# The opening of a three-stage kernel: the first block's words split in PSUM, eight weight tails by identity products, attention in finer stages

## The chip, the cores and the metric

The kernel runs on one core of a Trainium2 chip. Times are device microseconds of one launch. TensorE (PE in the profile), VectorE (DVE), ScalarE (ACT), GpSimd (POOL) and SyncE (SP, which only issues transfers here) each work through a queue of their own in order; semaphores hold an instruction until what it needs is there. The metric is the launch time, the median over several runs.

## The reference

```python
for t in range(S):                                       # B=4, H=8, S=768, D=48
    state = alpha[:, :, t, :, None] * state + einsum('bhd,bhe->bhde', k[:, :, t], v[:, :, t])
    y[:, :, t] = einsum('bhd,bhde->bhe', q[:, :, t], state)
x = y.transpose(0, 2, 1, 3).reshape(3072, 384)
out = 0                                                  # four experts, 384 -> 1024 -> 384
for e in range(4):
    out += (probs[:, e:e+1] / sum(probs)) * (maximum(x @ w1[e], 0) @ w2[e])
h = out @ w_in                                           # 384 -> 2048 -> 384
return (h - tanh(h)) @ w_out
```

A gated linear attention makes 3,072 rows of 384 features; four experts and then one larger layer are applied to every row. All of it is float32.

## The kernel before

**Words in two parts.** The large products run in a rounded 32-bit format, so every operand is split into a high part (the rounded word) and a low part (word minus high part), and a product is three: high by high, low by high, high by low. A weight tile of an expert (`w`, 128 by 768, one for each of the eight hidden slices f) is split by `w_prep`: ACT rounds it (line 425) and POOL subtracts (line 426). Attention's small products keep plain float32, which the trace records as two matmuls each.

**Attention.** Work is cut into 24 units (128 time steps of one batch entry). A unit is: two scans over the gates on DVE (`st_c`, line 260, and `st_r`, line 270), the scaled queries and keys (`st_prod`, 280), transposes and scores on PE (303 and 308), the key copy on ACT (315), the mask on DVE (322), the state update and the outputs on PE (333, 341, 344; the first four units have no state yet and use 348), the copy of the outputs (376), their store to DRAM as `xr` on ACT's queue (381), and the state's update on DVE and POOL (356, 358, 365, 367). `st_flag` takes a range check of the scans on ACT (290). A table, `STAGES`, gives each piece an offset; `points` walks through it, four points to a unit, and so writes the order in which the engines get the pieces.

**The first expert and the attention run together.** `steps0` is expert 0 over the rows in blocks: 256, 256, then five of 512. A step is one block and one f: `mm1` (line 589, 9 matmuls into `ph`), then ReLU and split by `evac1` (ACT 596, DVE 597), then `mm2` (line 641, 9 matmuls into three `po` banks), which is issued one step later (`flush(1)`). Between the two halves of a step the loop issues some points of attention, enough that the units of the next block are ready in time. `x_load` fetches a block of rows from DRAM (`xraw`), `x_parts` splits it on ACT and DVE (520, 521).

**The opening.** Before the loop: 20 matmuls on zeros (`busy`) keep PE occupied, units 0 and 1 run alone, their outputs go to DRAM by line 381 and come back as the first block. In between stand `w_prep(0)` to `w_prep(3)` and more `busy` matmuls; `w_prep(4)` to `w_prep(7)` are issued in the first four steps of the loop.

**The rest** (experts 1 to 3 in paired blocks, then the last layer) is not touched, but for one list that is emptied between the two (`phs`, which picks PSUM banks).

Of the kernel before, what the change touches and what calls it, by code (L numbers as in the profile page):

```python
# [183 lines left out]
def tile_kernel(ctx: ExitStack, tc: tile.TileContext, qka, a0, v, vT, pT, w12, w64, out):  # L184
# [34 lines left out]
    ident = const.tile([112, 112], F32, name="ident", tag="ident")  # L219
# [53 lines left out]
    def st_scan(u):  # L273
        st_c(u)
        st_r(u)

# [21 lines left out]
    def st_scores(u):  # L298
        s = unit[u]
        if u < NU - B:  # L300
            s["pt"] = bank(u, [P, 448], 0)
            for j in range(4):
                nc.tensor.transpose(s["pt"][:, j * 112:(j + 1) * 112],  # L303
                                    s["prod"][:, 512 + j * C:512 + (j + 1) * C], ident)
# [21 lines left out]

    def st_out(u):
        s = unit[u]
        heads = [(j, hf, r, slice((2 * j + hf) * D, (2 * j + hf + 1) * D)) for j in range(4) for hf, r in halves()]
        if u < NU - B:  # L330
            s["pu"] = bank(u, [112, 4, D], 0)
            for j, hf, r, h_ in heads:
                nc.tensor.matmul(s["pu"][r, j], s["kt"][:, j * 112 + 64 * hf:j * 112 + 64 * hf + D], s["vt"][:, h_],  # L333
                                 start=True, stop=True)
# [10 lines left out]
        else:  # L345
            for j, hf, r, h_ in heads:
# [3 lines left out]
    def st_upd(u):  # L350
        s = unit[u]
        if u < NU - B:
            for hf, r in halves():
# [3 lines left out]
                else:  # L357
                    nc.vector.tensor_copy(sd, s["pu"][r])
# [10 lines left out]
    def st_y(u):  # L369
        s = unit[u]  # L370
        s["y"] = at.tile([112, 512], F32, name="y", tag="y", bufs=2)
        for hf, r in halves():
            if u < 2 and hf:
                nc.vector.tensor_copy(s["y"][r], s["py"][r])
            else:
                nc.scalar.copy(s["y"][r], s["py"][r])

    def st_store(u):
        s = unit[u]
        for hf, r in halves():  # L380
# [5 lines left out]
    STAGES = [(st_out, 9), (st_scores, 3), (st_kt, 4), (st_mask, 4), (st_upd, 10), (st_y, 10), (st_store, 10),  # L386
              (st_state, 11), (st_scan, 0), (st_prod, 1), (st_flag, 2), (st_load, 2)]
# [12 lines left out]
    def ready(u):  # L400
        return 4 * (u - 2) + 11
# [21 lines left out]
    def w_parts(w, t):  # L423
        wh, wl = (w[:, k].rearrange("p a n -> p (a n)") for k in range(2))
        nc.scalar.copy(wh, t)
        nc.gpsimd.tensor_tensor(out=wl, in0=t, in1=f32(wh), op=ALU.subtract)
# [75 lines left out]
    blocks0 = [(0, 256), (256, 256)] + [(t, 512) for t in range(512, NT, 512)]  # L502
# [20 lines left out]
    def x_keep(t0, n):  # L523
        o, i = t0 % 512, t0 // 512
        nc.sync.dma_start(out=xs[i][:, :, i % 2:, o:o + n], in_=f32(xt[0, t0][:, :, i % 2:, :n]))
# [225 lines left out]
    with tc.manual_schedule():  # L751
        a_load(0)
        qk_load(0)
        nc.sync.dma_start(out=a0s, in_=a0)
        a_load(1)
        v_load(0)
        qk_load(1)
        w_load(0)
        v_load(1)
# [4 lines left out]
        v_load(2)  # L764
        w_load(3)
        a_load(3)
        qk_load(3)
        v_load(3)
        pr = at.tile([P, NE, 24], F32, name="pr", tag="pr")
        nc.sync.dma_start(out=pr, in_=pT.rearrange("e (p j) -> p e j", p=P))  # L770
        w_load(4)
# [13 lines left out]
        make_identity(nc, ident)  # L785
        make_upper_triangular(nc, mask)
        for t in state + sbd:
# [18 lines left out]

        st_c(0)
# [3 lines left out]
        w_prep(0)  # L811
        st_scores(0)
        st_kt(0)
        st_mask(0)
# [10 lines left out]
        busy(4)  # L825
        st_out(1)
        st_y(1)
        st_store(1)
        x_load(0, 0, 256)
        w_load(5)  # L830
        w_load(6)
        w_load(7)
        st_upd(0)
        st_upd(1)
        st_flag(0)
        busy(10)
        points(2)
        st_flag(1)
        w_prep(2)
        for kb in range(KB):  # L840
            x_parts(0, 256, kb)
        points(3)
        w_prep(3)
# [212 lines left out]
```

## Time and profile before

| | |
|---|---|
| runs | 1322.45, 1323.63, 1318.81 us (median 1322.45) |
| profiled execution, its own time | 1320.48 us |
| its span, first to last instruction | 1318.7 us |
| busy: PE, DVE, ACT, POOL | 97%, 69%, 46%, 41% |
| TensorE clock granted, mean | 0.986 of full speed |

A `PE` row is matrix work, `PEld` a weight load beside it. The granted clock is the share of full speed that TensorE was given: 1.00 is 2.4 GHz and 0.50 is 1.2 GHz, its two levels. Rows of the timeline merge instructions of one kind; what stands in square brackets is how long the engine had been idle before the row, and on what.

### The profile page before, as it was taken

The page shows a single profiled execution, that of the slowest core. Times are in us where ns is not written, and L with a number is a line of the kernel's source. Part 1 is how long each engine was busy: PE and PEld are TensorE (multiplying, and loading weights), DVE is VectorE, ACT ScalarE, POOL GpSimd, SP SyncE. Part 2 cuts the span into 40 slices and gives each one's busy share as a digit, 9 for nine tenths or more (in the row PEclk, how much of TensorE's full clock was granted, in tenths as well). Part 3 has the DMA queues.
Part 4 walks back from the last instruction along what each step waited for, and adds up shares of the span by engine and source line. Part 5 has one row for each costly group of instructions (what it writes and reads, how often), then busy time and mean ns, then how long its engine had stood idle before and what let it go on. Part 6 is the DMA issues. An engine that isn't in the chain of part 4 may idle for free.

```text
span 1318.7 us, 18568 instructions
## 1 busy us (share of the span) xinstructions
PE 1285.5 (97%) x6748; PEld 1051.6 (80%) x6748; DVE 906.7 (69%) x1383; ACT 610.0 (46%) x1096; POOL 536.8 (41%) x487
## 2 busy tenths in 40 slices
PE   6799999999999999999999999999999999999997
PEld 3788888888788887888888888888888888888885
DVE  7678667624456767776667766655878787878785
ACT  3343333323443324333333433334776767677764
POOL 3311110003433225522134521215787776767664
PEclk8789999999999999999999999999999999999999
DMA  7465543425662636471626261519100000000000
GB/s 245 121 164 167 163 127 120 149 64 174 226 209 102 221 109 208 125 239 44 215 71 233 88 204 64 191 53 346 50 25 1 25 0 25 0 25 0 25 1 28
DMA packets 86389, 153.24 MB, mean 116 GB/s; under 512 B 7568, under 2 KB 43664, under 8 KB 86032
## 3 DMA queue, kind: packets, MB, share of 16 engines
q1 hardware_dynamic: 76304, 147.24, 33.8%
q10 hardware_dynamic: 9984, 4.72, 1.4%
q8 instruction: 55, 0.90, 0.3%
q14 instruction: 46, 0.38, 0.1%
HBM read 115.71 MB, written 36.23 MB: 115 GB/s over the span
## 4 chain that ended last, share of the span: by engine, by line
PE 88%; DVE 4%; issue 2%; DMA 2%; ACT 1%; POOL 1%; SPq 0%; DVEq 0%; POOLq 0%; ACTq 0%
PE po L641 42%; PE ph L674 20%; PE ph L589 20%; PE pa L308 2%; PE pa L341 1%; PE pa L344 1%; DVE fg L260 1%; DMA xt<-xs 1%; PE pa L303 1%; DMA xraw<-xr 1%; PE pa L333 1%; DVE hl L597 0%; DVE prod L280 0%; DMA wraw<-w 0%; DVE fg L270 0%
## 5 line engine op out<-in xcount | busy, mean ns | idle before, releaser
L641 PE MATMUL po<-hh,w 128*128 128x512 f32 (+1 forms) x1776 | 450.5, 389 | 0.0
L641 PEld LDWEIGHTS po<-hh,w 128*128 128x128 f32 x1776 | 327.3, 189 | 73.9 <-issue 3.5
L589 PE MATMUL ph<-xt,w 128*128 128x512 f32 (+1 forms) x1368 | 327.0, 385 | 0.3 <-DVE ptmp L663 0.3
L589 PEld LDWEIGHTS ph<-xt,w 128*128 128x128 f32 x1368 | 251.9, 192 | 52.7 <-issue 1.2
L641 PE MATMUL po<-hl,w 128*128 128x512 f32 (+1 forms) x888 | 247.2, 386 | 1.2 <-DVE hl L621 1.2
L674 PE MATMUL ph<-xt,w 128*128 128x512 f32 x864 | 233.9, 392 | 1.3 <-DVE hl L597 0.9
L641 PEld LDWEIGHTS po<-hl,w 128*128 128x128 f32 x888 | 165.3, 189 | 35.8 <-DVE hl L621 1.6
L674 PEld LDWEIGHTS ph<-xt,w 128*128 128x128 f32 x864 | 162.4, 188 | 37.7 <-DVE hl L597 1.3
L597 DVE SCALAR_TENSOR_TENSOR hl<-ph,hh 128x512 fp32r<-128x512 f32 (+1 forms) x128 | 84.1, 657 | 143.8 <-ACT hh L596 143.7
L596 ACT ACTIVATE hh<-ph 128x512 fp32r<-128x512 f32 (+1 forms) x128 | 73.2, 572 | 237.0 <-PE ph L589 143.5
L75 POOL TENSOR_SCALAR gmk<-gu 128x512 int32<-128x512 f32 x96 | 143.3, 1493 | 48.8 <-ACT gu L71 48.1
L621 POOL TENSOR_TENSOR hl<-gg,hh 128x512 fp32r<-128x512 f32 x94 | 122.0, 1298 | 54.1 <-ACT hh L619 54.1
L479 POOL TENSOR_TENSOR wo<-wf,wo 128x384 fp32r<-128x384 f32 x32 | 35.1, 1098 | 211.1 <-ACT wo L478 211.1
L702 ACT COPY ut<-ph 128x512 f32<-128x512 f32 x108 | 63.4, 587 | 112.9 <-PE ph L674 112.5
L71 ACT ACTIVATE gu<-ph 128x512 f32<-128x512 f32 x96 | 57.7, 601 | 114.7 <-PE ph L589 69.7
L667 POOL TENSOR_TENSOR acc<-acc,ptmp 128x512 f32<-128x512 f32 x51 | 64.9, 1297 | 112.3 <-DVE ptmp L663 112.3
L674 PE MATMUL ph<-xt,ws 128*128 128x512 f32 x324 | 104.6, 395 | 1.2 <-DVE ph L736 1.2
L76 DVE SCALAR_TENSOR_TENSOR ghu<-ph,gu 128x512 f32<-128x512 f32 x96 | 66.3, 690 | 54.2 <-ACT gt L72 53.8
L80 DVE COPY_PREDICATED gg<-gmk,ph 128x512 f32<-128x512 int32 x96 | 71.9, 749 | 10.1 <-POOL gmk L75 0.3
L365 POOL TENSOR_TENSOR state<-state,fc 112x192 f32<-112x192 f32 x20 | 10.1, 506 | 168.6 <-DVE state L356 145.0
L79 DVE SCALAR_TENSOR_TENSOR gg<-gs,ghu 128x512 f32<-128x512 f32 x96 | 66.4, 692 | 12.7
L674 PEld LDWEIGHTS ph<-xt,ws 128*128 128x128 f32 x324 | 60.9, 189 | 15.8 <-DVE ph L736 2.3
(121 smaller groups left out, 1524.5 us busy)
## 6 DMA issues: line engine op xcount, KB each, us to landing
xt<-xs SPq DMA_DIRECT2D x54, 512.0 KB, 6.1
xt<-xb SPq DMA_DIRECT2D x27, 512.0 KB, 5.8
r<-w SPq DMA_DIRECT2D x32, 384.0 KB, 5.8
w64s<-wo SPq DMA_DIRECT2D x32, 384.0 KB, 3.1
w<-w64s SPq DMA_DIRECT2D x16, 768.0 KB, 6.3
qk<-qka SPq DMA_DIRECT2D x24, 448.0 KB, 6.3
wraw<-w SPq DMA_DIRECT2D x26, 384.0 KB, 3.9
pb<-pn SPq DMA_DIRECT2D x23, 256.0 KB, 4.4
```

The costliest lines, as they stand in the source:

```text
L75: nc.gpsimd.tensor_scalar(out=mk, in0=u, scalar1=T2, scalar2=None, op0=ALU.is_gt)
L76: nc.vector.scalar_tensor_tensor(out=hu, in0=ph, scalar=C4, in1=u, op0=ALU.mult, op1=ALU.mult)
L79: nc.vector.scalar_tensor_tensor(out=gg, in0=s2, scalar=B2, in1=hu, op0=ALU.add, op1=ALU.mult)
L80: nc.vector.copy_predicated(out=gg, mask=mk, data=ph)
L589: nc.tensor.matmul(ph[:, :n], w[:, a, 0, kb * P:(kb + 1) * P], x[:, b, kb, :n], start=m == 0, stop=m == len(seq) - 1)
L596: nc.scalar.activation(a[:, :n], ph[:, :n], AF.Relu)
L597: nc.vector.scalar_tensor_tensor(out=b[:, :n], in0=ph[:, :n], scalar=0.0, in1=f32(a[:, :n]), op0=ALU.max, op1=ALU.subtract)
L621: eng.tensor_tensor(out=b, in0=gg, in1=f32(a), op=ALU.subtract)
L641: nc.tensor.matmul(po[d, pool][:, :n], w[:, wi, 1, d * P:(d + 1) * P], r[:, :n], start=first and pi == 0, stop=last_ and pi == 2)
L667: nc.gpsimd.tensor_tensor(out=a_, in0=a_, in1=tmp, op=ALU.add)
L674: nc.tensor.matmul(ph, w[:, a], x[:, b], start=start and m == 0, stop=m == len(seq) - 1, skip_group_check=not start)
L702: nc.scalar.copy(t, ph)
```

## The change

Six edits, all in the opening and in the loop of expert 0:

1. The outputs of units 0 and 1 no longer go through DRAM before the first block. `place` copies parts of the values into a zeroed area (five small copies on ACT for a unit), so that `direct` can form the outputs with ten products whose rows are already in the order of the features; ACT rounds them out of PSUM into the high part, DVE subtracts into the low part, ACT copies them once more for the store that a later stage needs.
2. The low part of the eight weight tiles of expert 0 is made on PE: for each half of a tile, identity by the plain tile plus minus-identity by the high part, summed in PSUM; ACT copies the sum out. The POOL subtraction goes. `w_prep(0)` to `w_prep(2)` come before the loop, the other five in its first five steps.
3. The stages of attention are finer: the two scans stand at points 0 and 2 instead of both at 0, the products at 3, and everything behind one point later.
4. The blocks of expert 0 are four of 256 rows and four of 512; `mm2` is issued two steps behind `mm1`.
5. Small work moves: the gate of a unit's state (`fc`) from DVE to POOL, the first state copies from DVE to ACT, all output copies to ACT.
6. Loads are put in another order: the last four weight tiles are asked for before the loop, the row weights (`p_load`) in step 3, and rows are kept by one transfer for each of three parts.

```diff
-            nc.vector.tensor_tensor(out=s["fc"], in0=s["fg"].rearrange("p (j t) -> p j t", t=C)[:, 0:4, C - 1],
+            nc.gpsimd.tensor_tensor(out=s["fc"], in0=s["fg"].rearrange("p (j t) -> p j t", t=C)[:, 0:4, C - 1],
...
-                    nc.vector.tensor_copy(sd, s["pu"][r])
+                    nc.scalar.copy(sd, s["pu"][r])
...
+    def direct(u):
+        s = unit[u]
+        vz = spare(u * 480, 480)
+        py = bank(u, [P, 384], 1)
+        seen = {}
+        for (kb, h), (row, o) in PLACES.items():
+            a, b = max(48 * h, P * kb), min(48 * h + 48, P * kb + P)
+            w = s["vt"][:, a:b] if o is None else vz[:, o:o + (P if row == 0 else b - P * kb - row)]
+            n = seen[kb] = seen.get(kb, 0) + 1
+            nc.tensor.matmul(py[row:row + w.shape[1], kb * C:(kb + 1) * C], w,
+                             s["am"][h % 2][:, h // 2 * C:(h // 2 + 1) * C],
+                             start=n == 1, stop=True, skip_group_check=n > 1)
+        t = xt[0, 0][:, :, :, u * C:(u + 1) * C]
+        p3 = py.rearrange("p (k t) -> p k t", t=C)
+        nc.scalar.copy(t[:, 0], p3)
+        nc.vector.tensor_tensor(out=t[:, 1], in0=p3, in1=f32(t[:, 0]), op=ALU.subtract)
+        y = spare(960, 384).rearrange("p (k t) -> p k t", t=C)
+        nc.scalar.copy(y, p3)
+        nc.scalar.dma_start(out=xr[0].rearrange("(kb p) t -> p kb t", p=P)[:, :, u * C:(u + 1) * C], in_=y)
...
-    STAGES = [(st_out, 9), (st_scores, 3), (st_kt, 4), (st_mask, 4), (st_upd, 10), (st_y, 10), (st_store, 10),
-              (st_state, 11), (st_scan, 0), (st_prod, 1), (st_flag, 2), (st_load, 2)]
+    STAGES = [(st_out, 10), (st_scores, 4), (st_kt, 5), (st_mask, 5), (st_upd, 11), (st_y, 11), (st_store, 11),
+              (st_state, 12), (st_c, 0), (st_r, 2), (st_prod, 3), (st_flag, 3), (st_load, 3)]
...
-            w_parts(w, wraw.pop(i))
+            t = wraw.pop(i)
+            wh, wl = (w[:, k].rearrange("p a n -> p (a n)") for k in range(2))
+            nc.scalar.copy(wh, t)
+            for o in (0, 384):
+                pw = rolling(0)
+                nc.tensor.matmul(pw[:, 0:384], ident, t[:, o:o + 384], start=True, stop=False)
+                nc.tensor.matmul(pw[:, 0:384], negid, wh[:, o:o + 384], start=False, stop=True)
+                nc.scalar.copy(wl[:, o:o + 384], pw[:, 0:384])
...
-    blocks0 = [(0, 256), (256, 256)] + [(t, 512) for t in range(512, NT, 512)]
+    blocks0 = [(t, 256) for t in range(0, 1024, 256)] + [(t, 512) for t in range(1024, NT, 512)]
...
-        st_out(0)
-        st_y(0)
-        st_store(0)
+        update(0)
+        direct(0)
         st_scores(1)
         st_kt(1)
+        w_prep(0)
         st_mask(1)
-        w_prep(1)
-        busy(4)
-        st_out(1)
-        st_y(1)
-        st_store(1)
-        x_load(0, 0, 256)
...
+        st_flag(0)
+        points(3)
+        update(1)
+        direct(1)
+        w_prep(1)
+        st_flag(1)
+        points(4)
         st_upd(0)
         st_upd(1)
...
-        busy(10)
...
+        w_prep(2)
...
-            flush({5: 2, 6: 3, 7: 3}.get(f, 1) if last else 1)
+            flush({5: 2, 6: 3, 7: 3}.get(f, 1) if last else 2)
...
-                if bi == 0 and f < 4:
-                    w_prep(4 + f)
+                if bi == 0 and f < 5:
+                    w_prep(3 + f)
```

How PE's queue changes where the loop begins. First the kernel before: the last transposes and scores ahead of the loop (`pa` is an attention bank), then both first steps' `mm1` (18 matmuls into `ph`), then the first `mm2` into the `po` banks.

```order
L303 MATMUL pa<-ident,prod 128x112 x4
L308 MATMUL pa<-prod 128x128 x8
L589 MATMUL ph<-xt,w 128x256 x18
L641 MATMUL po_481<-hh,w 128x256
L641 MATMUL po_482<-hh,w 128x256
L641 MATMUL po_483<-hh,w 128x256
```

The same place in the changed kernel (`acc_88` and `acc_89` are where the plain weight tiles wait, line 631 is `mm1`, 300 and 305 are the transposes and scores):

```order
L463 MATMUL ph<-acc_88,ident 128x384
L464 MATMUL ph<-w,negid 128x384
L463 MATMUL ph<-acc_88,ident 128x384
L464 MATMUL ph<-w,negid 128x384
L631 MATMUL ph<-xt,w 128x256 x9
L300 MATMUL pa<-ident,prod 128x112 x4
L305 MATMUL pa<-prod 128x128 x8
L463 MATMUL ph<-acc_88,ident 128x384
L464 MATMUL ph<-w,negid 128x384
L463 MATMUL ph<-acc_88,ident 128x384
L464 MATMUL ph<-w,negid 128x384
L631 MATMUL ph<-xt,w 128x256 x9
```

The products that make the low parts of a weight tile now stand in PE's queue ahead of each early `mm1`, and the first `mm2` has gone back behind the third `mm1`.

How ACT's queue changes between the second unit's outputs and the first ReLU. Before (425 rounds a weight tile, 290 is the range check, 520 rounds the rows that came back from DRAM, 596 is the ReLU):

```order
L376 COPY y<-pa 48x512
L381 DMA xr_91<-y 48x4x128 x2
L290 ACTIVATE ab,flags<-fg 112x1024 x2
L425 CAST w<-acc_88 128x768
L520 CAST xt<-xraw 128x256 x3
L290 ACTIVATE ab,flags<-fg 112x1024
L425 CAST w<-acc_88 128x768
L596 ACTIVATE hh<-ph 128x256
```

After (410 and 413 read unit 1's outputs out of PSUM, 459 rounds a weight tile, 465 copies half a low part out of PSUM, 361 are state copies, 638 is the ReLU):

```order
L410 CAST xt<-pa 128x3x128
L413 COPY acc_87<-pa 128x384
L414 DMA xr_91<-acc_87 128x3x128
L459 CAST w<-wraw 128x768
L465 CAST w<-ph 128x384 x2
L287 ACTIVATE ab,flags<-fg 112x1024 x2
L361 COPY state_136<-po_286 48x192 x2
L361 COPY state_137<-pa 48x192 x2
L459 CAST w<-acc_88 128x768
L465 CAST w<-ph 128x384 x2
L638 ACTIVATE hh<-ph 128x256
```

The wait for the rows from DRAM (520) is gone from ACT's queue; in its place stand two low-part copies for each weight tile, the second copy of the outputs and four state copies, all ahead of the first ReLU.

## Rows read from the trace of the kernel before

**Rows 1.** The page, busy time, share of the span and instructions of PE (first engines of the line).

```profile
PE 1285.5 (97%) x6748; PEld 1051.6 (80%) x6748; DVE 906.7 (69%) x1383; ACT 610.0 (46%) x1096; POOL 536.8 (41%) x487
```

**Rows 2.** Busy time by stretch: length, PE, PEld, DVE, ACT, POOL, clock, DMA.

```profile
10.00:20.00 10.00, 7.33 (x73) 4.69 (x72) 6.60 (x7) 2.69 (x5) 3.62 (x2) 0.71 1.05 325
20.00:30.00 10.00, 3.88 (x36) 2.24 (x32) 7.39 (x11) 5.50 (x11) 2.77 (x1) 0.84 0.46 140
33.40:82.05 48.65, 38.89 (x329) 35.41 (x327) 30.96 (x56) 16.05 (x32) 12.56 (x19) 0.78 0.53 145
90.00:1318.00 1228.00, 1217.15 (x6170) 996.24 (x6167) 844.15 (x1276) 578.89 (x1037) 510.68 (x446) 1.00 0.33 111
```

**Rows 3.** Timeline of PE around the first block: start, length, work, [idle before].

```profile
33.40 4.21 PE L589 MATMUL ph<-xt,w 128*128 128x256 f32 x18
...
43.39 0.98 PE L303 MATMUL pa<-ident,prod 112*128 112x112 f32 x4 [4.45 <-DVE prod L280]
...
82.05 1.33 PE L589 MATMUL ph<-xt,w 128*128 128x256 f32 x9
```

**Rows 4.** The chain in order of time, full clock: start, length, engine, work.

```profile
97.36 0.39 PE pa L303 x4
97.75 1.09 PE pa L308 x16
98.84 1.26 PE po L641 x9
100.09 1.07 PE ph L589 x9
101.17 0.49 PE pa L333 x16
101.66 0.22 PE pa L341 x4
...
128.34 2.05 PE ph L589 x9
...
132.65 2.26 PE po L641 x9
```

**Rows 5.** Timeline of DVE and POOL about unit 1, as Rows 3.

```profile
9.19 0.18 DVE L266 RECIPROCAL r_end<-den 112x4 f32<-112x4 f32 x1
...
9.72 1.29 DVE L322 TENSOR_TENSOR am<-po,mask 128x512 f32<-128x512 f32 x2 [0.35 <-PE po L308]
...
10.50 1.81 POOL L426 TENSOR_TENSOR w<-wraw,w 128x768 fp32r<-128x768 f32 x1 [6.01 <-ACT w L425]
...
10.93 2.46 DVE L270 TENSOR_TENSOR_SCAN fg<-aa,r_end 112x512 f32<-112x512 f32 x1
...
13.43 1.22 DVE L280 TENSOR_TENSOR prod<-qk,fg 112x1024 f32<-112x1024 f32 x1
```

**Rows 6.** DVE by line and shape, 0 to 90 us: busy, mean ns.

```profile
L260 DVE TENSOR_TENSOR_SCAN fg<-aa,c_beg 112x512 f32<-112x512 f32 x8 | 12.5, 1564 | 1.7 <-DMA aa<-qka 1.6
L280 DVE TENSOR_TENSOR prod<-qk,fg 112x1024 f32<-112x1024 f32 x8 | 11.2, 1401 | 0.2
L270 DVE TENSOR_TENSOR_SCAN fg<-aa,r_end 112x512 f32<-112x512 f32 x8 | 11.0, 1379 | 0.2
...
L597 DVE SCALAR_TENSOR_TENSOR hl<-ph,hh 128x256 fp32r<-128x256 f32 x10 | 4.2, 418 | 16.2 <-ACT hh L596 16.2
```

**Rows 7.** ACT by line and shape, 0 to 90 us, as Rows 6.

```profile
L290 ACT ACTIVATE ab<-fg 112x1024 bf16<-112x1024 f32 x8 | 8.4, 1056 | 7.3 <-DVE fg L270 5.0 <-DVE y L374 1.1 <-DVE sm L798 0.4
...
L425 ACT CAST w<-acc 128x768 fp32r<-128x768 f32 x6 | 5.0, 825 | 0.0
L596 ACT ACTIVATE hh<-ph 128x256 fp32r<-128x256 f32 x10 | 3.8, 384 | 25.1 <-PE ph L589 25.1
...
L290 ACT ACTIVATION_READ_ACCUMULATOR ab<-fg 112x1 f32 x8 | 1.5, 186 | 0.0
```

**Rows 8.** Timeline, issue of two stores on ACT's queue.

```profile
65.57 0.92 ACTq L381 DMA_DIRECT2D xr<-y  x2
```

More of the change, by code (lines that the diff above doesn't have):

```diff
@@ L210, in tile_kernel @@
     w64s = [dr.tile([P, 2, 2, 384], F32, name=f"w64s{i}", tag=f"w64s{i}") for i in range(16)]
-    ident = const.tile([112, 112], F32, name="ident", tag="ident")
+    ident = const.tile([P, P], F32, name="ident", tag="ident")
+    negid = const.tile([P, P], F32R, name="negid", tag="negid")
     mask = const.tile([P, C], F32, name="mask", tag="mask")
@@ L325, in st_mask, with heads, update @@
             s["am"].append(am)
+    def heads(u):
+        return [(j, hf, r, slice((2 * j + hf) * D, (2 * j + hf + 1) * D)) for j in range(4) for hf, r in halves()]
+    def update(u):
+        s = unit[u]
+        if u < NU - B:
+            s["pu"] = bank(u, [112, 4, D], 0)
+            for j, hf, r, h_ in heads(u):
+                nc.tensor.matmul(s["pu"][r, j], s["kt"][:, j * 112 + 64 * hf:j * 112 + 64 * hf + D], s["vt"][:, h_],
+                                 start=True, stop=True)
     def st_out(u):
         s = unit[u]
[L329 to L334, printed above, removed]
+        update(u)
         s["py"] = bank(u, [112, 512], 1)
@@ L345, in st_out @@
         else:
-            for j, hf, r, h_ in heads:
+            for j, hf, r, h_ in heads(u):
                 t_ = slice(j * C, (j + 1) * C)
@@ L372, in st_y, with spare, place @@
         for hf, r in halves():
[L373 to L376, printed above, removed]
+            nc.scalar.copy(s["y"][r], s["py"][r])
+    PLACES = {(0, 1): (0, 0), (0, 0): (0, None), (0, 2): (96, None),
+              (1, 3): (0, 128), (1, 2): (0, None), (1, 4): (64, None), (1, 5): (96, 384),
+              (2, 6): (0, 256), (2, 5): (0, None), (2, 7): (64, 416)}
+    def spare(o, n):
+        return acc[0].rearrange("p k t -> p (k t)")[:, o:o + n]
+    def place(u):
+        vz = spare(u * 480, 480)
+        for (kb, h), (row, o) in PLACES.items():
+            if o is not None:
+                a, b = max(48 * h, P * kb), min(48 * h + 48, P * kb + P)
+                o += a - P * kb - row
+                nc.scalar.copy(vz[:, o:o + b - a], unit[u]["vt"][:, a:b])
+    def direct(u):
+        s = unit[u]
+        vz = spare(u * 480, 480)
+        py = bank(u, [P, 384], 1)
+        seen = {}
+        for (kb, h), (row, o) in PLACES.items():
+            a, b = max(48 * h, P * kb), min(48 * h + 48, P * kb + P)
+            w = s["vt"][:, a:b] if o is None else vz[:, o:o + (P if row == 0 else b - P * kb - row)]
[10 more added lines that the diff above has]
+        nc.scalar.dma_start(out=xr[0].rearrange("(kb p) t -> p kb t", p=P)[:, :, u * C:(u + 1) * C], in_=y)
     def st_store(u):
@@ L524, in x_keep @@
         o, i = t0 % 512, t0 // 512
-        nc.sync.dma_start(out=xs[i][:, :, i % 2:, o:o + n], in_=f32(xt[0, t0][:, :, i % 2:, :n]))
+        for k in range(i % 2, KB):
+            nc.sync.dma_start(out=xs[i][:, :, k, o:o + n], in_=f32(xt[0, t0][:, :, k, :n]))
     def form_load(p, h):
@@ L764, in tile_kernel @@
         v_load(2)
+        nc.sync.dma_start(out=a0s, in_=a0)
         w_load(3)
@@ L805, in p_norm @@
             nc.sync.dma_start(out=pn.rearrange("e (p j) -> p e j", p=P), in_=pr)
+        xt[0, 0] = xp.tile([P, 2, KB, 512], F32R, name="xt", tag="xt")
         st_c(0)
@@ L810, in tile_kernel @@
         st_c(1)
-        w_prep(0)
+        place(0)
         st_scores(0)
         st_kt(0)
+        place(1)
         st_mask(0)
-        busy(4)
+        busy(5)
         st_r(1)
         st_prod(1)
-        st_out(0)
-        st_y(0)
-        st_store(0)
+        update(0)
+        direct(0)
         st_scores(1)
         st_kt(1)
+        w_prep(0)
         st_mask(1)
+        st_flag(0)
+        points(3)
+        update(1)
+        direct(1)
         w_prep(1)
-        busy(4)
-        st_out(1)
-        st_y(1)
-        st_store(1)
-        x_load(0, 0, 256)
-        w_load(5)
-        w_load(6)
-        w_load(7)
+        st_flag(1)
+        points(4)
         st_upd(0)
         st_upd(1)
-        st_flag(0)
-        busy(10)
[L837 to L843, printed above, removed]
-        points(4)
         st_state(0)
         st_state(1)
+        w_prep(2)
         conv = [(i, hf) for i in range(16) for hf in range(2)]
@@ L930, in tile_kernel @@
                 x_keep(t0, n)
+                if not last:
+                    p_load(*nxt)
         pair_tile(2)
@@ L971, in tile_kernel @@
             pass
+        phs.clear()
         mid.close()
```

27 lines of the change are left out of this document (12 added, 15 removed).

## The prediction

> **What bounds the kernel now.** The page's busy times come first: PE is busy 97% of the span [rows 1], so one asks where the rest is. The table by stretch answers: from 90 us on PE is busy 1217.15 of 1228.00 us at a granted clock of 1.00, but between 10 and 30 us the clock is 0.71 and 0.84 and PE has little to do, and in the 48.65 us of the first block it is busy 38.89 us at a clock of 0.78 [rows 2]. A change of the opening is therefore worth what it does to one moment, the start of the second block's first `mm1`, at 82.05 us [rows 3], plus what matrix work it adds behind it; from there on PE hardly waits.
>
> What that block is made of follows from single pieces at full clock [rows 4]: transposes 0.39 and scores 1.09, `mm1` 1.07, `mm2` 1.26, state update 0.49, outputs eight pieces of 0.22 (the first four units, without a state, half of that). Between 33.40 and 82.05 us stand 8 `mm1` (8.56), 7 `mm2` (8.82), four units' transposes and scores (5.92), the updates and outputs of units 2 and 3 (2.74) and of unit 4 (2.25): 28.3 us. The block took 48.65. PE waited 48.65 - 38.89 = 9.8 us, and 38.89 - 28.3 = 10.6 us went to running at 1.2 instead of 2.4 GHz. The waits are for DVE; the longest is 4.45 us, on `prod` [rows 3], and after it the clock is at half.
>
> **The change part by part.** Start of the first block. Before, it waits for the round trip through DRAM until 33.40. Now it waits for ACT. I follow the queue at full clock. The masks of unit 0 end at 9.72 + 1.29 = 11.0 [rows 5]. `direct(0)` has ten float32 products of 128 columns, two passes each. A pass costs 0.22 / 4 = 0.055 (the narrow output products) to 0.39 / 4 = 0.098 for 112 columns, so 0.112 for 128 (the transposes) [rows 4]: 1.1 to 2.2 us, and I take 2.0, since the wide ones cannot lie side by side. That is 13.0. DVE meanwhile scans and multiplies (1.23, half of the 2.46 shown, and 1.22 [rows 5]) until 13.5; transposes and scores of unit 1 run to 15.0.
>
> ACT needs about 0.5 for 384 columns and 0.55 for 448 (between 0.384 for 256 and 0.825 for 768 [rows 7]). It rounds the outputs to 13.5; DVE subtracts, behind `prod`, to 14.0; ACT copies for the store to 14.5, issues it (0.46 [rows 8]) to 15.0, copies the keys to 15.5 and rounds weight tile 0 to 16.35. Then PE does minus-identity, identity, minus-identity.
>
> The price of an identity product of 384 columns: no row shows one. Two passes at 0.098 per 112 columns give 0.67, two at 0.055 per 128 give 0.33. I take 0.67, because the transposes are the only rows where all 128 columns of the array are loaded and nothing lies beside. The minus-identity product is in the rounded format: 0.17, between 1.07 / 9 for 256 columns and 2.05 / 9 for 512 [rows 4]. Three of them: 1.03, to 17.4. ACT copies the low part (0.5) and takes the range check (1.06 + 0.19 [rows 7]) to 19.15. PE updates and forms unit 1's outputs (0.49 + 2.0) to 19.9.
>
> DVE cannot start unit 2 before the check: 19.15 + 1.23 + two small operations (0.18 each [rows 5]) + 1.23 = 22.0, then subtracts unit 1's low part to 22.5, so ACT's second copy ends at 23.0, the issue at 23.5, weight tile 1 at 24.3, its low part on PE at 25.3, its copy at 25.8. Two range checks (2.5) make it 28.3, four state copies (1.3 at about 0.33 each, scaled from 0.384 for 256 columns) 29.6, weight tile 2 30.45, its products 31.5: first `mm1` at 31.5 at full clock. At half clock the three low parts (1.03 each) and unit 1's outputs cost 3.9 more: 35.4. The old kernel had 0.71 and 0.84 here [rows 2] and PE still waits twice for some 4 us (19.9 + 0.67 to 24.3, and 26 to 30.45), so I take the middle, 33.5. Taking the DRAM trip away is worth almost nothing: the wait for it becomes a wait for ACT.
>
> First block. PE's work: 8 `mm1` 8.56; 6 `mm2` 7.56 (one fewer, `mm2` runs two behind); transposes and scores of five units 7.4; outputs 2.74 + 2.25 as before; five weight tiles at 2 x (0.67 + 0.17) = 1.68, so 8.4. Sum 36.9, against 28.3. Waits at full clock, found by laying the queues side by side: tile 4's products wait for ACT's rounding of tile 4, which stands behind a ReLU and unit 3's range check, which needs a scan that DVE has behind the split of step 1: 0.38 + 0.42 + 1.23 + 1.25 + 0.83 = 4.1 [rows 6, 7], less 0.67 that PE has to do, 3.5. The transposes of units 4 and 5 wait 0.7 and 0.8 for `prod`, those of unit 6 some 2.8, behind the split of the next block's rows. Together 7.8. Half clock: two of these are long where three were before, so two thirds of 10.6, 7.1; the ends are 0 and 10.6 x 36.9 / 28.3 = 13.8. The block ends at 33.5 + 36.9 + 7.8 + 7.1 = 85.3, which is 3.25 later than 82.05.
>
> Behind it. One `mm2` more is still pending (1.26), and two blocks of 256 in place of one of 512 cost 16 x (1.07 + 1.26) - 8 x (2.05 + 2.26) = 2.8 [rows 4]: 4.1 us on a PE that has no slack.
>
> The rest. The POOL products of the weight tiles go (1.81 each [rows 5]); nobody is short of POOL here, but they held DVE up: the three largest DVE steps average 1.56, 1.40 and 1.38 over 8 each [rows 6], where 1.22 is what `prod` takes with POOL idle [rows 5]: 8 x (0.34 + 0.18 + 0.16) = 5.5 us, which is in the sum, since I used undisturbed times. Moving `fc` to POOL and state and output copies to ACT takes under 1 us off DVE and puts it on queues that have room after the opening. The reordered loads are ahead of their use; one that came late would cost its own landing, and one that now comes early gains at most the 10.85 us that PE lacks after 90 us [rows 2]; I put 0.
>
> Sum: 3.25 + 4.1 = +7.35. The profiled execution took 1320.48 us of its own time (span 1318.7 and 1.8 around it), 2.0 below the median of the runs, 1322.45. So 1327.8 for a like execution, and 1329.8 for the median: 0.56% slower.
>
> **The rivals.** *DVE was what held the block, and freed of POOL it holds nothing.* The Trainium skill, "SBUF — State Buffer", section "Who interferes with whom", says that DVE and GpSimd share one port pair under an exclusive lock, and the loser waits for the whole instruction; the scan of 2.46 beside a POOL product of 1.81 agrees. As a mechanism of this kernel: the 5.5 us and the finer stages feed PE without gaps, and a gapless PE keeps 2.4 GHz. Then 31.5 + 36.9 = 68.4, 13.65 earlier, less 4.1: -9.55, 1312.9. For it: all long waits name DVE. Against: five tiles' chains through ACT remain, and the wait of 3.5 runs through both. It decides if PE waits under 2 us in the block. Chance 0.20.
>
> *The identity products keep the clock up.* Waits as forecast, no half clock: 31.5 + 36.9 + 7.8 = 76.2, 5.85 earlier, less 4.1: -1.75, 1320.7. For it: PE has something to do nearly all the time. Against: two waits of 4 us before the block. With identity products at 0.33 instead, the forecast loses 13 x 0.34 = 4.4: 1325.4. Chance of the two 0.24.
>
> *PE at half clock throughout the block.* If weight tiles and attention lose as large a share as the old block did, 48.65 / 28.3 = 1.72, it lasts 63.4, ends at 96.9: +14.85 + 4.1 = +18.95, 1341.4. It decides if ACT's chain opens a gap in each of the five steps with a tile. Chance 0.14.
>
> **How the numbers follow.** The forecast has 0.42 and its own range 1324 to 1337 (start 31.5 to 35.4, half clock 4 to 11). Half a percent, 6.6 us, is about what a measurement of this kernel can tell from no change. The forecast lies just past it: of its 0.42, 0.28 is slower and 0.14 same; the half-clock case is slower; the middle rivals are same; the first is faster but for 0.02, and I add 0.06 to faster and take it from the middle for waits that I have laid out too long. That is 0.24 faster, 0.34 same, 0.42 slower. The range, 1311 to 1340, leaves out the far halves of the outer cases.
>
> **What would show it.** First `mm1` of the block between 31.5 and 35.4 us with ACT's rounding of tile 2 as what PE waited for; each identity pair 0.84 us at full clock; first `mm1` of the second block near 85 us; 37 us of work in the block and a wait of 3 us or more ahead of its third `mm1`. It is wrong if the second block starts before 78 us, if an identity product takes 0.35 us, or if PE waits over 15 us after 90 us.

## The result and the profile after

The changed kernel took 1327.59 us (median of 7 runs, 1326.92 to 1329.63), the kernel before, run beside it, 1320.55 (7 runs, 1317.74 to 1323.63): ratio 1.0056, 95% interval 1.0042 to 1.0071. It is 0.6% slower. The profiled execution is the slowest of the seven (1329.63 us of its own time, span 1327.8). In it `mm1` is L631, `mm2` L683, the transposes L300, the scores L305, `direct`'s products L405, the identity product L463, minus-identity L464, ACT's rounding of a weight tile L459.

Busy time by stretch (columns as in [rows 2], whose stretches these answer to; the first block is now 36.46 to 83.10):

```profile
10.00:20.00 10.00, 9.06 (x73) 5.14 (x73) 5.49 (x7) 3.00 (x8) 0.35 (x2) 1.00 1.05 321
20.00:30.00 10.00, 7.20 (x44) 3.98 (x42) 4.49 (x6) 4.18 (x9) 0.20 (x1) 0.91 1.03 308
30.00:36.46 6.46, 2.90 (x7) 1.47 (x6) 0.00 (x0) 4.70 (x11) 2.38 (x6) 0.50 0.09 32
36.46:83.10 46.64, 39.33 (x370) 32.83 (x369) 28.57 (x50) 24.50 (x50) 9.60 (x13) 0.98 0.46 129
83.10:90.00 6.90, 6.90 (x75) 6.58 (x74) 2.87 (x5) 0.38 (x1) 0.34 (x2) 0.77 0.11 42
```

The first block starts 3.06 us later than the 33.40 of [rows 3] and lasts 46.64 us, 2.01 less than before; PE works about as long as before (39.33 and 38.89 us), but on more work at a clock of 0.98, where it was 0.78. DVE does nothing at all from 30 us to the block's start.

Timeline of PE, from the opening into the block and about the second block's start (columns as in [rows 3]):

```profile
11.53 0.49 PE L405 MATMUL po<-am,acc 128*128 128x128 f32 x2
...
15.18 0.60 PE L300 MATMUL pa<-ident,prod 112*128 112x112 f32 x4
...
27.70 0.44 PE L464 MATMUL ph<-w,negid 128*128 128x384 f32 x1 [2.80 <-ACT w L459]
...
34.37 0.69 PE L464 MATMUL ph<-w,negid 128*128 128x384 f32 x1 [3.56 <-ACT w L459]
34.86 1.48 PE L463 MATMUL ph<-acc,ident 128*128 128x384 f32 x2
35.56 1.09 PE L464 MATMUL ph<-w,negid 128*128 128x384 f32 x1
36.46 2.12 PE L631 MATMUL ph<-xt,w 128*128 128x256 f32 x9
...
39.99 0.91 PE L463 MATMUL ph<-acc,ident 128*128 128x384 f32 x2
40.45 0.63 PE L464 MATMUL ph<-w,negid 128*128 128x384 f32 x1
40.92 0.81 PE L463 MATMUL ph<-acc,ident 128*128 128x384 f32 x2
41.27 0.64 PE L464 MATMUL ph<-w,negid 128*128 128x384 f32 x1
41.74 1.24 PE L631 MATMUL ph<-xt,w 128*128 128x256 f32 x9
...
47.01 0.45 PE L464 MATMUL ph<-w,negid 128*128 128x384 f32 x1 [3.38 <-ACT w L459]
...
81.40 0.57 PE L300 MATMUL pa<-ident,prod 112*128 112x112 f32 x4 [1.90 <-DVE prod L277]
...
83.10 2.29 PE L631 MATMUL ph<-xt,w 128*128 128x256 f32 x9
```

Rows overlap, because matmuls are pipelined, so a price is read from start to start: an identity pair takes 0.93 and 0.82 us (39.99, 40.92, 41.74). The two waits of 2.80 and 3.56 us ahead of the block and the one of 3.38 ahead of its third `mm1` are all for ACT's rounding of a weight tile. In the first of them ACT itself had been held up by a transfer: before it may copy unit 1's outputs, the store of unit 0 has to leave their common buffer (timeline of ACT):

```profile
25.85 0.48 ACT L413 COPY acc<-pa 128x384 f32<-128x384 f32 x1 [1.28 <-DMA xr<-acc]
```

What ACT did in the longest of them stands in the chain of waits, in order of time (start, length, engine, work):

```profile
30.05 1.06 ACT ab L287 x2
...
31.12 1.15 ACT ab L287 x2
32.27 0.20 ACT state L361
...
33.49 0.84 ACT w L459
```

Two range checks (L287) and four state copies (L361, one of them shown) stand in ACT's queue between tile 1 and tile 2, as the forecast laid them out.

### The profile page after: what moved, and what is told of

Its sections match the earlier page's. It is cut to its first block, busy times and chain, and to the rows that moved or that the text cites. A ratio compares the mean times of both kernels' runs of the same rounds, so it can differ in the third digit from the quotient of the medians.

```text
span 1327.8 us, 19013 instructions
## 1 busy us (share of the span) xinstructions
PE 1296.3 (98%) x6935; PEld 1062.3 (80%) x6935; DVE 893.7 (67%) x1367; ACT 622.9 (47%) x1140; POOL 548.1 (41%) x500
## 4 chain that ended last, share of the span: by engine, by line
PE 87%; DMA 4%; DVE 3%; issue 2%; ACT 2%; POOL 1%; SPq 0%; DVEq 0%; ACTq 0%; POOLq 0%
PE po L683 41%; PE ph L716 20%; PE ph L631 20%; PE pa L305 2%; PE pa L344 1%; PE pa L347 1%; DMA xt<-xs 1%; PE ph L463 1%; DMA qk<-qka 1%; DMA aa<-qka 1%; DMA xt<-xb 1%; DMA wraw<-w 1%; PE pa L332 1%; PE pa L300 1%; DVE prod L277 0%
## 5 line engine op out<-in xcount | busy, mean ns | idle before, releaser
L683 PE MATMUL po<-hh,w 128*128 128x512 f32 (+1 forms) x1824 | 451.4, 383 | 0.0
L683 PEld LDWEIGHTS po<-hh,w 128*128 128x128 f32 x1824 | 331.5, 189 | 71.7 <-issue 3.0
L631 PE MATMUL ph<-xt,w 128*128 128x512 f32 (+1 forms) x1440 | 327.0, 372 | 0.0
L631 PEld LDWEIGHTS ph<-xt,w 128*128 128x128 f32 x1440 | 254.6, 190 | 50.6 <-issue 1.5
L683 PE MATMUL po<-hl,w 128*128 128x512 f32 (+1 forms) x912 | 248.0, 380 | 1.2 <-DVE hl L663 1.2
L683 PEld LDWEIGHTS po<-hl,w 128*128 128x128 f32 x912 | 167.1, 188 | 34.9 <-DVE hl L663 1.6
L368 POOL TENSOR_TENSOR state<-state,fc 112x192 f32<-112x192 f32 x20 | 27.6, 1379 | 132.6 <-DVE state L359 108.2
```

The costliest lines, as they stand in the source:

```text
L631: nc.tensor.matmul(ph[:, :n], w[:, a, 0, kb * P:(kb + 1) * P], x[:, b, kb, :n], start=m == 0, stop=m == len(seq) - 1)
L683: nc.tensor.matmul(po[d, pool][:, :n], w[:, wi, 1, d * P:(d + 1) * P], r[:, :n], start=first and pi == 0, stop=last_ and pi == 2)
```

## The experiments

How to read the results together: "second block" is the start of the second block's first `mm1` in the profile, 82.05 us before and 83.10 in the changed kernel. It comes from one profiled execution each, the median from 5 to 12 runs. Each kernel was timed against the kernel before on the same chip. Where an expectation names e2, e8, e9 or e11, these are numbers 2, 6, 7 and 10. "Edit 3" and the like mean a number of this list.

| kernel | second block | median us | ratio to before, 95% |
|---|---|---|---|
| changed kernel | 83.10 | 1327.59 | 1.0056 (1.0042 to 1.0071) |
| 1 POOL makes the low parts | 78.56 | 1320.68 | 0.9997 (0.9988 to 1.0006) |
| 2 tile 2 first | 81.32 | 1325.55 | 1.0038 (1.0025 to 1.0051) |
| 3 old blocks | 86.50 | 1324.11 | 1.0026 (1.0016 to 1.0035) |
| 4 identity products in the kernel before | 84.56 | 1323.53 | 1.0019 (1.0009 to 1.0028) |
| 5 old stages | 87.07 | 1327.55 | 1.0051 (1.0037 to 1.0064) |
| 6 other order, identity products kept | 86.58 | 1327.47 | 1.0043 (1.0029 to 1.0057) |
| 7 other order, POOL, old blocks | 71.12 | 1309.47 | 0.9914 (0.9900 to 0.9927) |
| 8 as 7, with fillers | 72.84 | 1310.86 | 0.9920 (0.9906 to 0.9933) |
| 9 POOL and old blocks, changed order | 77.92 | 1318.41 | 0.9986 (0.9976 to 0.9996) |
| 10 as 7, range check and state copies earlier | 69.70 | 1307.92 | 0.9908 (0.9890 to 0.9925) |
| 11 as 10, with identity products | 83.70 | 1321.41 | 1.0003 (0.9992 to 1.0013) |
| 12 changed kernel, identity products twice | 90.85 | 1333.53 | 1.0105 (1.0086 to 1.0124) |

**1. POOL makes the low parts.** In `w_prep` of the changed kernel:

```diff
-            for o in (0, 384):
-                pw = rolling(0)
-                nc.tensor.matmul(pw[:, 0:384], ident, t[:, o:o + 384], start=True, stop=False)
-                nc.tensor.matmul(pw[:, 0:384], negid, wh[:, o:o + 384], start=False, stop=True)
-                nc.scalar.copy(wl[:, o:o + 384], pw[:, 0:384])
+            nc.gpsimd.tensor_tensor(out=wl, in0=t, in1=f32(wh), op=ALU.subtract)
```

> The changed kernel with one part undone: the low parts of expert 0's eight weight tiles come from the POOL subtraction again; everything else stays. Theory A (the identity products are matrix work that PE has to do on top, 8.4 us in the first block, and their chain through ACT delays its start): the block's first mm1 comes near 24 us instead of 36.5, PE's work in the block falls from about 37 to 28.5 us, waits and half clock eat part of it, and the time falls by 4 to 8 us against the changed kernel, to 1320 to 1324. Rival B (the identity products pay for themselves, since they keep the clock at 0.98 in the block, where the old kernel had 0.78): the granted clock in the block falls below 0.85, the second block starts no earlier than 82 us, and the time stays within 2 us of the changed kernel or rises.

1320.68: theory A holds, 7 us come back. The price of the identity products in this kernel is 7 us, though they are 13.4 us of work (16 pairs of 0.84). The block from 33.82 on (its first `mm1` had already run, at 22.71) shows both sides of it:

```profile
33.82:78.56 44.74, 35.00 (x310) 31.09 (x310) 34.66 (x49) 17.69 (x37) 22.63 (x21) 0.81 0.50 139
```

PE's work is less and its granted clock is 0.81, where the changed kernel had 0.98: that half of the rival came true. Of the 7 us, 4.5 show at the second block; the rest comes behind it.

**2. Tile 2 first.** `w_prep(2)` is moved ahead of unit 1's range check, the state copies and `points(4)`:

```diff
         w_prep(1)
+        w_prep(2)
         st_flag(1)
         points(4)
...
         st_state(1)
-        w_prep(2)
```

> The changed kernel with weight tile 2 split ahead of the two range checks and the four state copies on ACT, not behind them. Theory A, if the start of the first mm1 were what counts: it comes about 4 us earlier (32 to 33 us) and the time falls by 3 to 4 us. Theory A': the block behind it is paced by the chain ReLU, split, scan, range check, rounding of the next tile, and by the products of queries and keys on DVE; then the first mm1 comes 4 us earlier, the second block no more than 1 us earlier, and the time stays within 1.5 us.

1325.55, 2 us less. The first `mm1` comes at 31.62 in place of 36.46, but the second block at 81.32, so of 4.8 us only 1.8 reach it; the scores of a unit now wait 2.1 us for the state copies that stand behind tile 2. The truth lies between the two expectations.

**3. Old blocks.**

```diff
-    blocks0 = [(t, 256) for t in range(0, 1024, 256)] + [(t, 512) for t in range(1024, NT, 512)]
+    blocks0 = [(0, 256), (256, 256)] + [(t, 512) for t in range(512, NT, 512)]
```

> The changed kernel with expert 0's blocks as before (256, 256, then five of 512). Theory A counts 2.5 to 2.8 us of extra matrix work for splitting a block of 512 in two, and the waits and the slow stretch behind the first block come from the thin attention in blocks 2 and 3: the time falls by 3 to 5 us, to 1322.5 to 1324.5. Rival B: if the 4 us by which the part behind the first block grew more than forecast come from elsewhere (late transfers in the paired stage), the time falls by 2 to 3 us only, and the waits on those transfers stay.

1324.11, 3.5 us less, as expected. How long the work behind the second block's start takes is read from the single product that checks the flags, some 240 us later (rows by line: duration, first and last start); L962 in the changed kernel and in this one, L924 before:

```profile
L962 PE MATMUL ph<-ones,rs x2: 163/164/164, 326.3 to 326.3; 112*1 112x1 f32 x2
```

```profile
L924 PE MATMUL ph<-ones,rs x2: 163/164/164, 319.5 to 319.6; 112*1 112x1 f32 x2
```

```profile
L962 PE MATMUL ph<-ones,rs x2: 163/164/164, 324.8 to 324.8; 112*1 112x1 f32 x2
```

From the second block's start: changed kernel 326.3 - 83.10 = 243.2, before 319.5 - 82.05 = 237.5, old blocks 324.8 - 86.50 = 238.3. In these executions four blocks of 256 thus cost 4.9 us behind that start; the other 0.8 is what the rest of the change, the one `mm2` more that is pending among it, adds there. The 4.9 hold some 1.5 us of half clock: from 83.10 to 120 us the mean clock is 0.96 in the changed kernel, here 1.00 over the same stretch. The first block, in turn, holds the same instructions in both kernels and took 49.90 us here at a clock of 0.90, against 46.64 at 0.98. So a second block's start is only good to about 3 us, and what the blocks cost in all is better read from the medians: 3.5.

**4. Identity products alone**, put into the kernel before with everything else as it was (edit 1 the other way round, `ident` at 128 wide).

> The kernel before with the identity products alone (a full-size identity and its negative with them, and the list phs emptied between the stages): the low parts of the eight tiles on PE and ACT. Theory A: the first mm1 comes 4 to 7 us later than 33.4, the second block starts at 87 to 91 instead of 82 us, and the time rises by 7 to 12 us against the kernel before, to 1328 to 1332. Rival B (they free DVE from POOL by 5.5 us and keep the clock up): the granted clock in the block rises from 0.78 above 0.9 and the time is within 3 us of the kernel before.

1323.53, 2.7 us more: theory A falls here and the rival holds by its time (its clock just misses the 0.9 that it asked for). The block is 36.45 to 84.56:

```profile
36.45:84.56 48.11, 41.31 (x353) 34.65 (x351) 28.28 (x56) 20.70 (x42) 3.57 (x9) 0.89 0.52 139
```

against 48.65 us at 0.78 before [rows 2]: the block with five more tiles of matrix work is no longer, because PE waits less (6.8 us, was 9.8) and its clock is higher. Only the start, 36.45 against 33.40, is later. So one and the same edit costs 2.7 us in one opening and 7 in another; number 11 takes that up.

**5. Old stages** in the changed kernel (both scans in one stage, each stage a point earlier, as the lines of the diff show them on the minus side).

> The changed kernel with the attention stages of the kernel before (both scans of a unit in one stage, everything a point earlier), the rest as changed. Theory A, that the finer stages shorten PE's waits for DVE: undone, the third mm1's and the transposes' waits grow and the time is 0 to 3 us above the changed kernel, 1327.5 to 1330.5. Rival B, that they only put a unit's products later: 2 to 4 us below it, 1323.5 to 1325.5.

1327.55, the same as the changed kernel: the finer stages are worth nothing measurable here, at the lower end of theory A. The rival falls. The second block starts 4.0 us later than in the changed kernel, but 1.4 of that is left at the flags' product (327.7 against 326.3).

**6. Another order, identity products kept.** Unit 1's rows go to a buffer of their own (the one that the raw rows of later blocks use), tile 2 is rounded early, and the scans of unit 3 come ahead of the first `mm1`:

```diff
-        y = spare(960, 384).rearrange("p (k t) -> p k t", t=C)
+        yo = spare(960, 384) if u == 0 else at.tile([P, KB, 512], F32, name="xraw", tag="xraw")[:, 0, 0:384]
+        y = yo.rearrange("p (k t) -> p k t", t=C)
...
         w_prep(1)
+        w_prep(2)
...
         st_state(1)
-        w_prep(2)
+        points(8)
```

> The changed kernel with ACT's and DVE's queue of the opening in another order, no work less: the buffer for unit 1's rows is its own (no wait for unit 0's store), weight tile 2 is rounded ahead of two range checks and four state copies, and unit 3's scans and its product are done ahead of the first mm1. Theory A, that the order of ACT's queue and the scans of unit 3 behind the first step's low part set the start and the third mm1's wait: first mm1 at 31 to 33, the wait of 3.4 us ahead of the third mm1 under 1 us, second block's first mm1 4 to 7 us earlier than 83.1, time 1320.5 to 1323.5. Rival B, that the transfers (full until 29 us) and the lower clock behind them set it: within 1.5 us of the version with tile 2 first alone (1325.5).

1327.47: theory A falls. The rival is left open: the median is 1.9 us above edit 2, but the ratios, 1.0043 and 1.0038, have intervals that overlap almost wholly. The first `mm1` is at 38.00. PE's waits from 28 us to the second block (us in total, times, longest):

```profile
PE pa L305 <- ACT state L361: 3.2, 1, 3.2
PE ph L465 <- ACT w L460: 2.7, 1, 2.7
PE pa L300 <- DVE prod L277: 2.3, 2, 1.2
PE pa L332 <- ACT kt L312: 0.9, 1, 0.9
```

The longest is neither theory's: the scores of unit 2 now stand ahead of the first `mm1` and wait for the state copies, which ACT makes behind its range checks.

**7. The same order with POOL's low parts and the old blocks** (edits 1, 3 and 6 together).

> The changed kernel with POOL making the low parts, the blocks of the kernel before (256, 256, then 512) and the order of e8. Theory A, that the three gains add (7 for POOL's low parts, 3.5 for the blocks, 2 to 4 for the order): 1313 to 1316. Rival B, that what is freed comes back as half clock, as with POOL's low parts alone (block at 0.81): second block near 78 and 1316.5 to 1319.

1309.47, 18.1 us less than the changed kernel and 11 us less than before: more is won than the sum of theory A. Beside it **9**, edits 1 and 3 in the changed kernel's own order, tells where that comes from:

> The changed kernel with POOL's low parts and the old blocks only, in its own order. If the two gains add (7 and 3.5) and the order brought the other 8 us of e9: 1316 to 1318. If the order is worth as little here as it was with the identity products (e8, 2 us above e2), and the two gains together are more than their sum: 1309 to 1312.

1318.41. Edits 1 and 3 add (9.2 us of 10.5), and the order brings the other 9 us, though it brought nothing with the identity products. PE's waits up to 90 us (us in total, times, longest), of 9 and then of 7:

```profile
PE pa L300 <- DVE prod L277: 12.1, 5, 6.4
PE pa L305 <- ACT state L361: 4.2, 1, 4.2
```

```profile
PE pa L300 <- DVE prod L277: 5.6, 3, 3.2
PE pa L305 <- ACT state L361: 3.7, 1, 3.7
```

With POOL's low parts PE stands idle for attention (12.1 us), and the order halves that. The longest of these waits, 6.4 us, ends in the rows of the second block, which still come back from DRAM (L556 rounds them, L557 is the split). In 9, by engine:

```profile
71.10 1.02 ACT L556 CAST xt<-xraw 128x256 fp32r<-128x256 f32 x3 [7.46 <-DMA xraw<-xr]
71.53 1.10 DVE L557 TENSOR_TENSOR xt<-xraw,xt 128x256 fp32r<-128x256 f32 x3 [5.53 <-ACT xt L556]
75.00 0.98 PE L300 MATMUL pa<-ident,prod 112*128 112x112 f32 x4 [6.36 <-DVE prod L277]
```

DVE's queue has `prod` of the last unit behind that split. In 7, with one unit's attention done ahead of the loop, `prod` comes first, at 65.34, the split at 68.51, and neither ACT nor PE waits for the rows. The new buffer shows too: in 9 ACT waits 2.8 us for the store of unit 0, in 7 not at all. In the changed kernel the same wait for the rows costs PE only 1.90 us (81.40 above), so there the order has little to win, and it loses more at the scores of unit 2 (number 6).

**8. Fillers.** As 7, with `busy(8)` twice in PE's queue (behind `w_prep(2)` and behind `st_upd(1)`).

> The same as e9 with sixteen more warm-up products (bf16, 512 columns, 0.22 us each at full clock, results unused) in PE's queue in the two places of the opening where it waits. Theory A, that the half clock behind the waits is what is left to gain: clock of the first block over 0.95, 3 to 5 us below e9. Rival B, that the waits for DVE in the block set the time and a faster PE only waits longer: within 1 us of e9, or up to 3 us above it where the products delay PE's own work.

1310.86, within the noise of 7: rival B by its time. From 20 us to the first `mm1`, and in the block, of 7 and then of 8:

```profile
20.00:31.69 11.69, 4.78 (x31) 3.31 (x31) 6.38 (x10) 6.40 (x13) 6.26 (x9) 0.76 0.92 274
31.69:71.12 39.43, 33.21 (x319) 29.73 (x319) 31.23 (x45) 18.30 (x38) 22.57 (x21) 0.85 0.45 133
```

```profile
20.00:31.16 11.16, 7.46 (x49) 4.24 (x49) 5.81 (x8) 6.40 (x13) 5.91 (x7) 1.00 0.98 296
31.16:72.84 41.68, 34.72 (x320) 31.09 (x320) 31.82 (x47) 18.30 (x38) 23.17 (x24) 0.80 0.49 136
```

The fillers hold the clock at 1.00 up to the block and no longer. Nothing of PE's own stands between the two groups, so they ran as one piece, from 22 to 25.6 us, and left the next wait empty:

```profile
30.07 1.16 PE L305 MATMUL pa<-prod 48*128 48x128 f32 x14 [3.54 <-ACT state L361]
```

Right behind it the clock falls, to 0.52 from 31.16 to 38.09, and it is low until 44 us. So this run shows that fillers ahead of the last wait win nothing; fillers in that wait were not tried.

**10. Range check and state copies earlier.** As 7, with two more moves in ACT's queue:

```diff
         st_flag(0)
+        st_flag(1)
         points(3)
...
         direct(1)
+        st_upd(0)
+        st_upd(1)
         w_prep(1)
         w_prep(2)
-        st_flag(1)
         points(4)
-        st_upd(0)
-        st_upd(1)
```

> As e9 (POOL's low parts, old blocks), with ACT's queue of the opening in a better order still: unit 1's range check right behind unit 0's, the four state copies ahead of the rounding of weight tiles 1 and 2. Theory A, that in e9 the 3.7 us in which PE waits for the state copies and the 4.5 us in which DVE waits for unit 1's buffer (both behind ACT's range checks) still hold the first block: both gone, first mm1 near 28, 2 to 4 us below e9: 1305.5 to 1307.5. Rival B, that the raw weight tiles, which land until 29 us, hold it all the same: within 1 us of e9 (1309.5).

1307.92, the fastest, 1.6 us under 7 with intervals that overlap. The wait for the state copies is gone and the first `mm1` comes at 28.33 (31.69 in 7), yet the second block only 1.4 us earlier: the transposes of unit 3 now wait 3.0 us for `prod`.

**11. The same with identity products** prices them where PE waits least for anything else.

> As e11, but with the low parts by identity products as in the changed kernel. It prices them where PE waits least. Theory A, that their price is what PE's other waits do not hide, so that it grows as these go (2.7 us in the kernel before, 7 in the changed one): 12 to 18 above e11, 1318 to 1324. Rival B, that it is the same 7 as in the changed kernel: 1313 to 1315.

1321.41, 13.5 us above 10: theory A. Their price is 2.7, 7 and 13.5 us in the three openings. The block of 10, then of 11:

```profile
28.33:69.70 41.37, 33.48 (x319) 30.08 (x319) 30.84 (x45) 19.43 (x41) 26.33 (x27) 0.85 0.52 147
```

```profile
34.62:83.70 49.08, 41.71 (x351) 34.31 (x349) 25.46 (x45) 23.78 (x51) 7.74 (x12) 0.90 0.45 127
```

11 starts its block 6.3 us later and needs 7.7 us more for it: 8.2 us more of PE work, hardly fewer waits (7.4 against 7.9 us).

Side by side, from 10 us to the second block (busy and idle time and clock of PE; the last column is the part of the idle time that ends with ACT's rounding of a weight tile):

| kernel | low parts by | PE busy | PE idle | clock | for ACT's rounding |
|---|---|---|---|---|---|
| before | POOL | 53.02 | 19.03 | 0.76 | 0 |
| 4 | PE | 62.34 | 12.22 | 0.89 | 4.4 |
| 1 | POOL | 51.47 | 17.09 | 0.81 | 0 |
| changed | PE | 58.49 | 14.61 | 0.93 | 10.7 |
| 10 | POOL | 47.58 | 12.12 | 0.86 | 0 |
| 11 | PE | 61.87 | 11.83 | 0.91 | 7.1 |

Two things pay for the products' 13.4 us. They fill PE's waits for attention, but bring waits for ACT of their own, so the idle time falls by 6.8, 2.5 and 0.3 us. And the clock is higher with them, most where it was lowest, so the busy time grows by only 9.3 and 7.0 us in the first two openings, by 14.3 in the last. These are single executions, so the price in the medians is the surer number; how much of it is PE's work and how much ACT's two copies for each tile no run took apart.

**12. Identity products twice**, in the changed kernel, the first of each pair thrown away:

```diff
+                nc.tensor.matmul(pw[:, 0:384], ident, t[:, o:o + 384], start=True, stop=True)
                 nc.tensor.matmul(pw[:, 0:384], ident, t[:, o:o + 384], start=True, stop=False)
```

> The changed kernel with each of its sixteen identity products made twice (0.65 us each by the pair's 0.83 less 0.18 for minus-identity), so 10.4 us more of TensorE's work and nothing else. Theory A, that matrix work in this opening is paid in full: +8 to +12, 1336 to 1340. Rival B, that ACT's rounding and DVE hide most of it, since PE waits 7 us in the block for them: +2 to +5, 1330 to 1333.

1333.53, 5.9 us more, between the two expectations: a little over half of 10.4 us is paid. A product made twice starts 0.64 us after the first (45.14 and 45.78 in PE's timeline, at full clock). In the block, PE is busy 45.39 us, 6.06 more, of which five tiles' ten products are 6.4, at a clock that is a little higher; PE's waits in it stay (7.1 us, was 7.3).

```profile
38.38:90.85 52.47, 45.39 (x390) 36.66 (x389) 28.57 (x50) 24.43 (x50) 9.94 (x14) 0.99 0.42 118
```

So inside the block matrix work is paid in full, and what the opening's three tiles cost is partly hidden behind ACT (first `mm1` at 38.38, 1.9 us later for six products of 0.64). The second block starts 7.75 us later, more than the 5.9 of the medians.

## Why the prediction came out right

The time (1329.8 forecast, 1327.59 measured) and the sign are right, and the second block's start was forecast at 85.3 and came at 83.10. Most of the 2.2 us lies in the kernel before, whose median was 1322.45 when the forecast was made and 1320.55 beside the changed kernel; the increase was forecast at 7.35 and is 7.04. That is partly luck, since the terms err in both directions: the block starts 3.0 us later than forecast, PE is busy 4.7 us less in it (39.33 for 36.9 + 7.1), waits 0.5 less, and 1.6 us more come behind it.

- **Start of the first block: 33.5 forecast, 36.46,** outside its own bounds of 31.5 to 35.4. The mechanism was right: the last wait is for ACT's rounding of tile 2. The term that was mis-sized most is the ten products of `direct`, taken at 2.0 us within bounds of 1.1 to 2.2: for unit 0 they took 3.65, from 11.53 to 15.18, at full clock. That is 1.7 of the 3.0 us. Another 0.5 is that they start at 11.53 and not at 11.0, since unit 0's state update stands ahead of them and was not counted, and 0.7 is ACT's wait for unit 0's store (what is left of the 1.28 once unit 1's low part is done, at 25.16), which the forecast did not have. Unit 1's ten products took as long (20.34 to 23.98) but cost next to nothing: ACT has rounded their outputs at 24.57, and DVE's scans end only at 24.46. The allowance of 2.0 for half clock was about right, with 0.56 from 28 to 30 us and 0.50 from there to the block. The bounds came from passes of narrower or overlapping products; why these take nearly twice as long was not measured by itself.
- **The identity pair: 0.84 forecast, 0.82 to 0.93 at full clock.** Right; edit 12 gives 0.64 for the product by itself (0.67 forecast).
- **Waits in the block: 7.8 forecast, 46.64 - 39.33 = 7.3.** Right, and at their places: 3.38 ahead of the third `mm1` (3.5 forecast), 1.90 for the last transposes (2.8). What holds these up is not the split of the next block's rows alone: ACT waits 3.10 us for the rows to come from DRAM.
- **Half clock: 7.1 forecast, about 0.9 measured.** This step failed; its own range was 4 to 11. A mean clock of 0.98 over 46.64 us means 1.9 us at half clock, half of which is lost. The rest of 39.33 - 36.9 = 2.4 is work that was priced too low. I had scaled the old block's loss by its number of long waits. The rival on identity products named what the runs show: in the eight versions with identity products the first block's clock is 0.86 to 0.99, in the five with POOL's low parts 0.80 to 0.85, and 0.78 in [rows 2]. That is one execution each, and one kernel's block can differ: the same instructions had 0.98 in the changed kernel and 0.90 in edit 3. The rival of half clock throughout is out by the same rows. The rival on identity products failed on its result, since its block started 5.0 us later than the 31.5 that it took and had 2.4 us more of busy time than its 36.9.
- **Behind the second block's start: +4.1 forecast, 5.7 up to the flags' product.** Edit 3 gives the parts in these executions: 4.9 for the smaller blocks (2.8 forecast), 0.8 for the rest (1.26 forecast for the pending `mm2`). About 1.5 of the 4.9 is the half clock at the second block's start (0.77 in the stretch 83.10 to 90), which leaves 3.4, near the 3.5 of the medians. Another 2.4 us of this execution come after that product, where PE waits 2.2 us for a transfer (0.4 before); as edits 1 to 3 run that stage 0.9 to 1.5 us faster than the kernel before, I read it as one execution's own, and the median lies 2.0 below it.
- **DVE freed of POOL.** That POOL's products lengthen DVE's work was right: in edit 1 a backward scan that starts at 36.90, beside a POOL product that ends at 38.45, took 2.63 us, alone 1.22. (The Trainium skill, "SBUF — State Buffer", section "Who interferes with whom", says that the two share a port pair under an exclusive lock; the trace agrees.) That it is worth a gapless block was wrong: with POOL making the low parts again the kernel was 7 us faster, so the products on PE cost more here than DVE gained.
- "Taking the DRAM trip away is worth almost nothing" was said of the first block's start, which came 3.06 us later than before. With POOL's low parts and ACT's queue in another order the first `mm1` stands at 28.33 and the kernel is 0.9% faster than before (edit 10). No run has that order with the trip left in, so how much of it the trip is worth is not shown.

So of the change's parts, the identity products cost 7 us, the smaller blocks 3.5, the finer stages nothing that can be measured. With the first two undone (edit 9) what is left of the change is 2.1 us faster than the kernel before (ratio 0.9986, 0.9976 to 0.9996): a small gain that the two hid. That it comes from the split straight from PSUM is likely but not shown, since the pending `mm2`, the moved small work and the order of the loads were not undone. What stays open, too: the 9 us of the order with POOL's low parts were not divided among its three moves by runs; the traces name the wait for the second block's rows (6.4 us) and the wait for unit 0's store (2.8).

## What to carry to other kernels

The price of work put on the engine that bounds a kernel is not its duration, but what the engine's other waits and its clock do not give back, and the work can bring waits of its own: the same products cost 2.7, 7 and 13.5 us here, most where PE had the fewest other waits. That is three openings, not a law. Test a change of several parts by undoing each part, because a gain and two losses can look like one small loss. After a start is made earlier, look at the next common point: 4.8 us at the first `mm1` were 1.8 at the second block. And where a fast start uncovers a wait, follow it to its end: PE's wait for DVE in edit 9 was a transfer from DRAM, two queues away.

## What the runs showed of the hardware

More matrix work came with a higher granted clock: with 39.33 us busy in a block of 46.64 the mean was 0.98, in one of 44.74 with 35.00 busy 0.81. The share of busy time alone does not settle it, for the same instructions had a mean of 0.90 in another kernel's execution (edit 3). Sixteen products whose results nobody uses kept it at 1.00 in the opening (0.76 without) and won nothing: after the wait of 3.54 us behind them it was 0.52. A float32 product of 384 columns with a 128 by 128 identity took 0.64 us at full clock, and `direct`'s ten products of 128 columns 3.65.
